# Batch 0 of a fused attention and feed-forward kernel: strided reads for strided writes, fewer constant rows, spare TensorE products, and a new order of steps

## The chip, the cores and the metric

The kernel runs on one core of a Trainium2 chip. Its time is the device time of one execution in microseconds (us); the median of three runs is 301.95 us (301.75 to 302.35). The engines are TensorE (PE in the profile; its weight loads PEld), VectorE (DVE), ScalarE (ACT), GpSimd (POOL) and SyncE (SP, which only issues DMAs here).

## The reference

Four batches of eight heads, 768 positions and 64 features go through block-sparse attention, and its result through a feed-forward layer with softplus. Keys are taken in chunks of 32 (24 chunks). For each query an upper bound on its product with any key of a chunk is worked out from the chunk's smallest and largest key values; the six chunks with the largest bounds, among those not in the future, are kept, and ordinary causal softmax attention runs over them.

```python
k_min, k_max = min, max of k over each chunk of 32
ub = sum_d maximum(q * k_min, q * k_max)          # one bound per query and chunk
ub = where(causal, ub, -1e9); top = 6 largest
scores = where(in a top chunk and causal, scale * q @ k.T, -1e9)
attn = softmax(scores) @ v
x = attn as (3072 tokens, 512)
out = softplus(x @ w_in) @ w_out                  # 512 -> 2048 -> 512
```

The sum of maxima is the same as max(q, 0) times k_max plus min(q, 0) times k_min, and also as max(q, 0) times k_max plus max(-q, 0) times (-k_min).

## The kernel before, in words

The work is cut into units. A unit is a pair of heads of one batch. In batch 0 each pair is halved along the queries, so that the first results come sooner: units 0 to 3 are the first 384 queries of the four pairs, units 4 to 7 the second 384. Units 8 to 19 are whole pairs of batches 1 to 3.

A unit goes through these steps, and each step has a short name that the order of work uses:

- `L` loads q, k or v (SP's queue). `ck`, `cq`, `cv` cast them to bf16.
- `kt` and `qt` transpose k and q on TensorE into PSUM (batch 0 only; later batches use DMA transposes, `fk` and `fq`). For batch 0's k the positions arrive interleaved by four, and the transposed tile holds them as (t, s), where position is 4 s + t.
- `rg` reduces the transposed k to chunk maxima (`.0`) and minima (`.1`), L234; `pk` packs them for TensorE, L240. `qp` and `qn` make max(q, 0) and min(q, 0), L262.
- `kr` copies the transposed k of one head into the score operand `Kaug` (L248). In batch 0 this copy puts the positions back in order: it reads PSUM in one run and writes every fourth element of SBUF.
- `U` is TensorE's bound product (L278, L279) with the causal mask added (L281), `M` takes the eight largest per row (MAX8, L291), `T` writes the selection beside q (L299, L300).
- `a` (batch 0) transposes q together with its selection and copies both to the score operand `Qaug` (L312, L313), reading PSUM in one run and writing every third element. Later batches use `qr` and `s` (L267, L324).
- `S` is a group of score products (L362) with exp on ACT (L366) and a causal cut of the diagonal blocks on POOL (L369). A score operand has 128 rows: 64 of the data and 64 in which the selection meets constant rows in `Kaug`, which drive unselected chunks to a huge negative score.
- `V` multiplies with v (L383, PSUM tile `o_ps`), `n` divides by the row sum (reciprocal L394, product L395), `X` and `x` transpose and copy the result (L402, L410).
- `I` is one step of the first feed-forward product with softplus (tile `hp`, L421; tile `gT`, L429), `F` a quarter of the second (tile `op`, L437), `ob` its copy and store (L442, L444). `I0.0.3` is step 3 of the first half of batch 0; `w` loads the weights on POOL's DMA queue. `tE` and `tP` load the ACT table of exp or of softplus ahead of its use (L122); where the table does not fit the next function, a load is put in.

The letters V, A and G behind a step name the engine (DVE, ACT, POOL). The whole order is written out by hand as text: `ORDER["start"]` for batch 0 and the beginning of batch 1, and `ORDER["cycle"]`, which is run twice. Every engine and every DMA queue takes its instructions strictly in this order. PSUM has three kinds of buffers of two each: `ps_big` (scores and `hp`), `ps_sm` and `ps_w`.

Before the first step a block builds the constants: `aug` (64 rows that hold the chunk pattern, rows 25 to 63 zero) on DVE and POOL, the identity for transposes on POOL, the causal masks, and zeros and ones in several tiles on DVE. `aug_rows(i)` copies all 64 rows of `aug` by DMA, issued by ACT, into the constant half of the two `Kaug` tiles of pair i.

Of the kernel before, what the change touches and what calls it, by code (L numbers as in the profile page):

```python
# [21 lines left out]
L3.k L1.q L1.k L3.q ck1.G L0.k L0.q ck0.V cq1.V kt1.b cq0.V L2.v L3.v kt0 rg1.0 qt0 rg0.1 kr1.1.A qt1.b rg0.0 pk0  # L22
kr0.1.A qp0 rg1.1 L1.v qn0 pk1 qn1 L2.q U0 kr1.0.A kr0.0.A M0 L2.k T0 qp1 a0.1.V a0.0.A ck2.V L0.v U1 cq2.V ar1 cv0.G
M1 S0.0.0 S0.1.0 T1 kt2 cv1 rg2.1 ck3.V rg2.0 a1.0.V a1.1.A V0.0 qt2 V0.1 kr2.0.A cq3.A pk2 S1.0.0 n0.0 qp2 kr2.1.A
qn2 ar2 kt3 rg3.1 w0 L4.q U2 M2 n0.1 S1.1.0 V1.0 qt3 T2 ar3 kr3.0.A n1.0 rg3.0 a2.0.A a2.1.A qp3 cv2.A X0 w1 pk3 V1.1
x0 n1.1 kr3.1.A qn3 cv3 S2.0.0 S2.1.0 U3 M3 X1 L5.q T3 a3.0.A L6.q w2 L5.k x1.A ck5.V V2.0 n2.0 L4.k cq4.A V2.1 a3.1.V
n2.1 S3.0.0 qt4 ck4.V S3.1.0 V3.0 X2 n3.0 L6.k V3.1 x2.V tP n3.1 kt4 L4.v X3 x3.V I0.0.0 kr4.0.V L5.v I0.0.1 rg4.1
rg4.0 L7.q cq5.G w3 qn4 qp4 I0.0.2 pk4 ck6.G U4 L7.v kt5 rg5.1 I0.0.3 M4 kr4.1.V w4 T4 rg5.0 I0.0.4 cv4.V a4.0.V w5 tE
L8.k kr5.1.A kr5.0.A S4.0.0 qt5 kt6 pk5 L6.v qn5 qp5 cv5.V L7.k U5 M5 rg6.1 S4.0.1 a4.1.V I0.0.5 ck7 T5 cq6.G a5.1.V
z1 qt6 I0.0.6 kr6.1.V a5.0.A qp6 I0.0.7 rg6.0 pk6 qn6 L9.v z0 kr6.0.V U6 cq7.G S4.1.0 M6 T6 S4.1.1 V4.0 cv6.G L8.v  # L30
a6.1.V n4.0 L9.k S5.0.0 a6.0.V V4.1 n4.1 S5.0.1 kt7 qt7 cv8.G S5.1.0 rg7.0 L8.q rg7.1 X4 L9.q qn7 cv7.G V5.0 S5.1.1
kr7.0.A pk7 kr7.1.A qp7 n5.0 x4.A cq8.V S6.0.0 ck8.A L10.q U7 S6.0.1 M7 F0.0.0 T7 a7.0.V V5.1 S6.1.0 n5.1 a7.1.V
F0.0.1 S6.1.1 ck9.A F0.0.2 V6.0 S7.0.0 fk8 S7.0.1 cq9.A n6.0 V6.1 cv9.G rg8.0 X5 x5.A n6.1 L10.v L10.k tP F0.0.3 ob0.0
S7.1.0 fk9 V7.0 F0.1.0 n7.0 fq9 F0.1.1 X6 F0.1.2 S7.1.1 F0.2.0 rg9.1 F0.1.3 V7.1 fq8 x6.V ck10.G n7.1 L11.q X7 x7.A
F0.2.1 rg8.1 F0.2.2 qn8 qr9.1.V F0.2.3 I0.1.0 kr8.0.V qr8.0.G ob0.1.V fk10 L11.k qp8 pk8 L11.v U8 ob0.2.V kr8.1.A M8
cq10.V qr8.1.G cv10.V I0.1.1 qp9 kr9.1.G fq10 T8 I0.1.2 I0.1.3 cq11.G I0.1.4 qn9 L12.q cv11.V L12.k s8 I0.1.5 I0.1.6
I0.1.7 rg9.0 L12.v pk9 S8.0.0 qr9.0.V fq11 rg10.0 U9 ck11 tE S8.0.1 L13.k M9 T9 fk11 S8.0.2 rg10.1 L13.v ck12 s9 L13.q
kr10.0.A L14.q S8.1.0 kr9.0.A qp10 qn10 pk10 V8.0 F0.3.0 S8.1.1 U10 kr11.0.G M10 T10 n8.0 qr10.0.G S8.1.2 F0.3.1
S9.0.0 S9.0.1 V8.1 n8.1 cq12.A qr10.1 F0.3.2 cv12.G kr10.1.G rg11.0 S9.0.2 S9.1.0 s10 qr11.0.V rg11.1 X8 F0.4.0 L14.v
qn11 x8.A V9.0 kr11.1.A qp11 fk12 ck13 pk11 qr11.1.G S9.1.1 S9.1.2 n9.0 F0.3.3 fq12 U11 fk13 ob0.3.A M11 T11 L15.v  # L40
S10.0.0 V9.1 S10.1.0 n9.1 S10.0.1 s11 X9 cv13.V kr12.0.G qr12.0 qp12 rg12.0 rg12.1 L14.k S10.0.2 S10.1.1 qr12.1 pk12
V10.0 cq13.V S10.1.2 kr12.1.G L15.k S11.0.0 L15.q F0.4.1 S11.0.1 qn12 x9.V F0.4.2 fq13 S11.0.2 n10.0 U12 S11.1.0 V11.0
M12 S11.1.1 n11.0 V10.1 T12 F0.4.3 ck14.V S11.1.2 cq14.G n10.1 F0.5.0 s12 V11.1 F0.5.1 cv14.G tP n11.1 F0.5.2 X11 X10
F0.5.3 x11.V cv15.A ob0.4.A fk14 L16.q x10.V I1.-.0 I1.-.1 I1.-.2 qn13 rg13.0 I1.-.3 kr14.1.V fq14 L16.k L16.v I1.-.4
qp14 I1.-.5 rg14.1 qn14 qp13 ob0.5.A rg14.0 I1.-.6 I1.-.7 rg13.1 pk14 I1.-.8 kr13.0.V I1.-.9 cq15.A ck15.G qr14.1.V
# [12 lines left out]
M17 I2.-.10 I2.-.11 qn18 T17 I2.-.12 U18 kr18.0 I2.-.13 fq19 cv19.A I2.-.14 I2.-.15 L21.q M18 kr18.1.V tE T18 L21.k
s18 qr18.0.G L21.v s17
# [11 lines left out]
def kernel(  # L71
# [35 lines left out]
    aug = singles.tile([D, S], BF16, name="aug")  # L107
# [39 lines left out]

    def aug_rows(i):
        for e in range(2):
            nc.scalar.dma_start(out=Kaugs[2 * i + e][D * e:D * (e + 1), :], in_=aug)  # L150
# [66 lines left out]

    def k_turn(u, at=(ps_w, "w")):
        p, t0, t1 = units[u]
        st = state[u]  # L220
        st["kT"] = at[0].tile([128, (t1 - t0) * 128], BF16, name="kT", tag=at[1])
        r = (t1 - t0) * 32
        for t in range(4):
            nc.tensor.transpose(st["kT"][:, t * r:(t + 1) * r],
                                st["kb"][:, t].rearrange("p e d -> p (e d)"), ident[0:r, 0:r])

    def k_range(u, which):
# [6 lines left out]
        nc.vector.tensor_reduce(st["km2"][:, which, :], kT, axis=AX.XY, op=(ALU.max, ALU.min)[which])  # L234
# [7 lines left out]
    def k_rows(u, e, copy=nc.vector.tensor_copy):  # L242
# [3 lines left out]
        if t1 - t0 < NT:  # L246
            o, kT = o.rearrange("p (s t) -> p t s", t=4), kT.rearrange("p (t s) -> p t s", t=4)
        copy(o, kT)  # L248

    def q_turn(u, at=(ps_w, "w")):  # L250
        p, t0, t1 = units[u]
        st = state[u]
        st["qT"] = at[0].tile([128, (t1 - t0) * 128], BF16, name="qT", tag=at[1])
        for t in range(t1 - t0):
            nc.tensor.transpose(st["qT"][:, t * 128:(t + 1) * 128],
                                st["row"][:, t, 1:3, :].rearrange("p c d -> p (c d)"), ident)

    def q_sign(u, name):
# [3 lines left out]
        (nc.vector.tensor_scalar_max if name == "qpos" else nc.vector.tensor_scalar_min)(st[name], st["qT"], 0.0)  # L262
# [6 lines left out]
    def bounds(u):  # L269
# [4 lines left out]
        ub = ps_sm.tile([128, n, cs, 2], F32, name="ub", tag="sm")  # L274
# [218 lines left out]
    with tc.manual_schedule():  # L493
# [5 lines left out]
        for m in kmms:  # L499
            nc.vector.memset(m, 0.0)  # L500
# [52 lines left out]
```

## Time and profile before

| what | value |
|---|---|
| median of three runs | 301.95 us |
| the profiled execution: time, span | 301.01 us, 299.2 us |
| busy: PE, DVE, ACT, POOL | 260.1, 171.4, 197.9, 74.4 us |
| mean granted TensorE clock | 0.97 |
| chain that ended last: PE, DVE, ACT, DMA, issue | 62%, 17%, 10%, 5%, 3% of the span |
| first TensorE instruction | 6.92 us |
| first feed-forward product (`hp`) | 36.8 us |
| moved by DMA in the first 60 us | 12.30 MB, 205 GB/s |

How to read it: the page cuts the span into 40 slices of 7.5 us and gives each engine's busy share in tenths. The chain of work that ended last is followed back from the last instruction, at each step to what released it; a row of it in order of time is start, duration, and what ran. In a group by line, `out<-in`, partitions x elements and type are followed by the count, the busy time in us and the mean of one in ns, then the idle time before them and what ended it. A row of stretches is from:to, length, then busy time and count of PE, PEld, DVE, ACT and POOL, the granted TensorE clock (1 is full speed), the DMA share and GB/s.

### The profile page before, as it was taken

The page shows a single profiled execution, that of the slowest core. Times are in us where ns is not written, and L with a number is a line of the kernel's source. Part 1 is how long each engine was busy: PE and PEld are TensorE (multiplying, and loading weights), DVE is VectorE, ACT ScalarE, POOL GpSimd, SP SyncE. Part 2 cuts the span into 40 slices and gives each one's busy share as a digit, 9 for nine tenths or more (in the row PEclk, how much of TensorE's full clock was granted, in tenths as well). Part 3 has the DMA queues.
Part 4 walks back from the last instruction along what each step waited for, and adds up shares of the span by engine and source line. Part 5 has one row for each costly group of instructions (what it writes and reads, how often), then busy time and mean ns, then how long its engine had stood idle before and what let it go on. Part 6 is the DMA issues. An engine that isn't in the chain of part 4 may idle for free.

```text
span 299.2 us, 6118 instructions
## 1 busy us (share of the span) xinstructions
PE 260.1 (87%) x2407; PEld 162.0 (54%) x2432; DVE 171.4 (57%) x572; ACT 197.9 (66%) x244; POOL 74.4 (25%) x104
## 2 busy tenths in 40 slices
PE   0385795789898797799999999999999999999994
PEld 0263553456455464556666666556666655665441
DVE  4986477985485799985459684646494313000000
ACT  1588549899756797655768788765786774567100
POOL 5035412433410665171013324112032120000000
PEclk9996599999999799999999999999999999999999
DMA  7989999916769998519395731932000101000111
GB/s 187 208 202 190 240 201 197 214 37 132 169 103 243 208 199 187 123 53 192 90 182 84 176 101 24 187 101 51 2 3 35 72 2 70 35 2 0 70 72 70
DMA packets 93628, 35.26 MB, mean 118 GB/s; under 512 B 82336, under 2 KB 90528, under 8 KB 93600
## 3 DMA queue, kind: packets, MB, share of 16 engines
q1 hardware_dynamic: 88768, 29.89, 47.9%
q0 software_dynamic: 4192, 4.19, 8.7%
q10 hardware_dynamic: 640, 0.79, 1.1%
q8 instruction: 19, 0.31, 0.5%
q14 instruction: 9, 0.07, 0.1%
HBM read 27.26 MB, written 6.29 MB: 112 GB/s over the span
## 4 chain that ended last, share of the span: by engine, by line
PE 62%; DVE 17%; ACT 10%; DMA 5%; issue 3%; SPq 1%; POOL 0%; ACTq 0%; DVEq 0%
PE hp L421 23%; PE op L437 21%; PE sc L362 8%; PE o_ps L383 6%; ACT attnT L366 4%; DVE km L234 3%; DMA vf<-in_v_dram 3%; ACT Kaug L248 2%; DMA kf<-in_k_dram 2%; DVE m L291 2%; PE x_ps L402 1%; DVE on L395 1%; DVE Kaug L248 1%; DVE kmm L240 1%; DVE Qaug L313 1%
## 5 line engine op out<-in xcount | busy, mean ns | idle before, releaser
L366 ACT ACTIVATE attnT<-sc 128x1024 bf16<-128x1024 f32 (+2 forms) x96 | 84.6, 917 | 23.0 <-PE sc L362 21.9
L437 PE MATMUL op<-w_out_sb,gT 128*128 128x512 bf16 x360 | 88.6, 381 | 1.4 <-issue 0.2
L421 PE MATMUL hp<-xT,w_in_sb 128*128 128x384 bf16 x512 | 87.0, 328 | 1.3 <-ACT attnT L366 1.3
L429 ACT ACTIVATE gT<-hp 128x768 bf16<-128x768 f32 x64 | 51.9, 810 | 38.6 <-PE hp L421 38.5
L421 PEld LDWEIGHTS <-w_in_sb 128*128 128x128 bf16 x512 | 49.9, 99 | 34.2 <-issue 2.7
L369 POOL TENSOR_SCALAR_AFFINE_SELECT attnT<-attnT 128x768 bf16<-128x768 bf16 (+1 forms) x40 | 29.4, 737 | 121.2 <-ACT attnT L366 121.1
L362 PE MATMUL sc<-Qaug,Kaug 128*128 128x128 bf16 (+3 forms) x399 | 53.1, 266 | 3.6 <-ACT attnT L366 2.1
L437 PEld LDWEIGHTS <-gT 128*128 128x128 bf16 x384 | 36.0, 98 | 35.0 <-issue 0.6
L362 PEld LDWEIGHTS <-Kaug 128*128 128x128 bf16 x400 | 30.3, 102 | 17.5 <-issue 4.0
L383 PE MATMUL o_ps<-vaug,attnT 128*128 128x65 bf16 x672 | 28.9, 198 | 4.5 <-ACT Qaug L313 2.0
L442 DVE COPY ob<-op 128x512 f32<-128x512 f32 x14 | 9.6, 686 | 40.0 <-PE op L437 39.8
L383 PEld LDWEIGHTS <-attnT 128*128 128x128 bf16 x672 | 26.7, 100 | 10.6 <-issue 3.1
L234 DVE TENSOR_REDUCE km<-kT_sb 128x24 bf16<-128x768 bf16 x24 | 22.2, 946 | 3.4 <-DMA kT_sb<-kb 3.2
L324 DVE COPY Qaug<-sT 64x768 bf16<-64x768 bf16 x24 | 13.3, 553 | 13.6 <-PE sT L321 13.4
L395 DVE TENSOR_TENSOR on<-o_ps,rr 128x384 bf16<-128x384 f32 (+1 forms) x40 | 19.1, 478 | 1.4
L394 DVE RECIPROCAL rr<-o_ps 128x6 f32<-128x6 f32 (+1 forms) x40 | 7.4, 184 | 20.5 <-PE o_ps L383 20.3
L281 DVE TENSOR_TENSOR ubm<-ub,causal 128x288 f32<-128x288 f32 (+2 forms) x20 | 7.5, 380 | 18.5 <-PE ub L279 18.2
L442 ACT COPY ob<-op 128x512 f32<-128x512 f32 x10 | 5.9, 585 | 17.2 <-PE op L437 17.2
L248 ACT COPY Kaug<-kT 64x384 bf16<-64x384 bf16 x12 | 11.8, 1024 | 7.5 <-DVE km L234 7.3
L291 DVE MAX8 m<-ubm 128x8 f32<-128x12 f32 (+3 forms) x192 | 16.4, 160 | 0.5
L278 PE MATMUL ub<-kmm,qpos 128*128 128x48 bf16 (+1 forms) x96 | 7.8, 184 | 6.2 <-DVE kmm L240 2.2
L410 ACT COPY xT<-x_ps 128x768 bf16<-128x768 bf16 (+1 forms) x11 | 7.6, 689 | 7.5 <-PE x_ps L402 7.4
(69 smaller groups left out, 243.5 us busy)
## 6 DMA issues: line engine op xcount, KB each, us to landing
out_dram<-ob SPq DMA_DIRECT2D x24, 256.0 KB, 2.1
kf<-in_k_dram SPq DMA_DIRECT2D x12, 384.0 KB, 6.1
vf<-in_v_dram SPq DMA_DIRECT2D x12, 384.0 KB, 5.4
qf<-in_q_dram SPq DMA_DIRECT2D x12, 384.0 KB, 5.4
w_in_sb<-in_moe_w_in_dram POOLq DMA_DIRECT2D x4, 512.0 KB, 8.0
w_out_sb<-in_moe_w_out_dram POOLq DMA_DIRECT2D x2, 1024.0 KB, 16.5
kf<-in_k_dram SPq DMA_DIRECT2D x8, 192.0 KB, 4.2
qf<-in_q_dram SPq DMA_DIRECT2D x8, 192.0 KB, 4.2
```

The lines of the kernel that those rows point to most:

```text
L234: nc.vector.tensor_reduce(st["km2"][:, which, :], kT, axis=AX.XY, op=(ALU.max, ALU.min)[which])
L248: copy(o, kT)
L291: nc.vector.max(out=m8[:, t, e, :], in_=ubm[:, t, 0:max(8, 4 * (t + 1)) if n == NT else cs, e])
L362: nc.tensor.matmul(sc[:, o:o + (z - a) * 128], pair[p]["Ka"][e][:, tj * 128:(tj + 1) * 128], pair[p]["Qa"][e][:, a * 128:z * 128], start=T ...
L366: nc.scalar.activation(at[:, g * 1024:g * 1024 + n], sc[:, 0:n], ACT.Exp, scale=scale)
L369: nc.gpsimd.affine_select(out=diag, in_=diag, compare_op=ALU.is_ge, fill=0.0, base=0, channel_multiplier=-1, pattern=[[0, t1 - t0], [1, 128]])
L383: nc.tensor.matmul(o_ps[:, t, :], at[:, o:o + 128], pair[p]["va"][:, tj, e, :], start=(tj == 0), stop=(tj == t0 + t))
L395: nc.vector.tensor_tensor(st["on"][:, :, e, :], o_ps[:, :, 0:D], rr.to_broadcast([128, n, D]), op=ALU.mult)
L421: nc.tensor.matmul(hp[:, n, 0:HALF], w_in_sb[:, dt, ft * 128:(ft + 1) * 128], xT[b][:, dt, half * HALF:(half + 1) * HALF], start=(dt == 0) ...
L429: nc.scalar.activation(o, hp[:, :, 0:HALF], ACT.Softplus)
L437: nc.tensor.matmul(held[b, stt], gT[b][:, ft, stt * 128:(stt + 1) * 128], w_out_sb[:, ft, :], start=(ft == 0), stop=(ft == KFF - 1))
L442: copy(ob, held.pop((b, stt)))
```

## The change

- The two strided copies of batch 0 are turned round: they write SBUF in one run and read PSUM with jumps (`kr`: 96 elements between neighbours; `a`: 128 elements).
- `aug` has 32 rows, of which 25 go to `Kaug` by DMA; the rest of the constant half is zeroed by a POOL memset before each DMA.
- Minima are negated in the reduce, and `qn` makes max(-q, 0), so that both signs can also run on ACT as a Relu (`qp7.A`, `qn11.A` and others).
- `D n.m` adds n to a counter, and the next PSUM tile that TensorE starts (`kT`, `qT`, `ub`, `qa_ps`, `sc`, `o_ps`, `x_ps`) is first written by that many products of the identity with itself, transposes where the tile is bf16. There are 140 of them: 49 ahead of the first transpose of k, none in `ORDER["cycle"]`.
- Several steps name the PSUM buffer that they use (`.s`, `.w`, `.b`).
- The constants become steps (`C`), and the whole order of steps is written anew, loads included (`L1.q L1.k L0.k` first, where it was `L3.k L1.q L1.k`).

```diff
-L3.k L1.q L1.k L3.q ck1.G L0.k L0.q ck0.V cq1.V kt1.b cq0.V L2.v L3.v kt0 rg1.0 qt0 rg0.1 kr1.1.A qt1.b rg0.0 pk0
...
+L1.q L1.k L0.k Ci Ca Cr1.V cq1.V ar0 Cc Cr0.V L0.q L1.v Cv.V ck1.G D48.2 cq0.V D1.16 ck0.V L3.q kt1.b L3.k kt0 L2.v
...
+cv2.G pk3 a2.0.A.s D1.19 X0 x0.A V1.1.s qp3.V n1.1 w1 D1.22 qn3 L6.q kr3.1.A D1.31 S2.0.0 S2.1.0 D1.28 D6.40 U3.s M3
+D1.27 X1.b x1.A L5.q w2 D9.26 T3 D13.21 D1.30 cv3 L5.k D1.29 a3.0.A L4.k S3.0.0 L6.k ck5.V V2.0 V2.1 a3.1.V.w n2.0
...
+kr4.0.V I0.0.1 L5.v L7.q rg4.1 cq5.G I0.0.2 ck6.V qp4 L8.k w3 qn4 L6.v pk4 U4.s kt5 cv4.V D1.39 kr5.1.A I0.0.3 kr4.1.V
+L7.v rg5.1 tE M4 I0.0.4 w5 T4 D1.48 qt5 rg5.0 L7.k a4.0.V.s S4.0.0 qn5.V kr5.0.A S4.0.1 w4 cv5.V D1.41 kt6 qp5.V pk5
...
-    aug = singles.tile([D, S], BF16, name="aug")
+    aug = singles.tile([32, S], BF16, name="aug")
...
     def aug_rows(i):
         for e in range(2):
-            nc.scalar.dma_start(out=Kaugs[2 * i + e][D * e:D * (e + 1), :], in_=aug)
+            nc.gpsimd.memset(Kaugs[2 * i + e][D * e:D * (e + 1), :].bitcast(F32), 0.0)
+        for e in range(2):
+            nc.scalar.dma_start(out=Kaugs[2 * i + e][D * e:D * e + NCH + 1, :], in_=aug[0:NCH + 1, :])
...
+    def keep_busy(ps):
+        n = min(128, ps.shape[1])
+        for _ in range(spare[0]):
+            if ps.dtype == BF16:
+                nc.tensor.transpose(ps[:, 0:128], ident, ident)
+            else:
+                nc.tensor.matmul(ps[:, 0:n], ident, ident[:, 0:n], start=True, stop=True)
+        spare[0] = 0
...
-        nc.vector.tensor_reduce(st["km2"][:, which, :], kT, axis=AX.XY, op=(ALU.max, ALU.min)[which])
+        nc.vector.tensor_reduce(st["km2"][:, which, :], kT, axis=AX.XY, op=(ALU.max, ALU.min)[which],
+                                negate=which == 1)
...
-            o, kT = o.rearrange("p (s t) -> p t s", t=4), kT.rearrange("p (t s) -> p t s", t=4)
+            o, kT = o.rearrange("p (s t) -> p s t", t=4), kT.rearrange("p (t s) -> p s t", t=4)
...
+        sign = 1.0 if name == "qpos" else -1.0
+        if on == "A":
+            nc.scalar.activation(st[name], st["qT"], ACT.Relu, scale=sign)
+        elif sign > 0:
+            nc.vector.tensor_scalar_max(st[name], st["qT"], 0.0)
+        else:
+            nc.vector.tensor_scalar(st[name], st["qT"], -1.0, 0.0, ALU.mult, ALU.max)
...
-        copy(Qa[e][:, t0 * 128:t1 * 128].rearrange("p (s t) -> p t s", t=t1 - t0),
-             qa_ps.rearrange("p (t s) -> p t s", t=t1 - t0))
+        copy(Qa[e][:, t0 * 128:t1 * 128].rearrange("p (s t) -> p s t", t=t1 - t0),
+             qa_ps.rearrange("p (t s) -> p s t", t=t1 - t0))
```

## The prediction, made before the changed kernel ran

> **What bounds the kernel now.** I read the page's slices first, then stretches of the span, then the chain of work that ended last, then the groups by line with the shapes kept apart. On the page:
>
> ```profile
> span 299.2 us, 6118 instructions
> PE 260.1 (87%) x2407; PEld 162.0 (54%) x2432; DVE 171.4 (57%) x572; ACT 197.9 (66%) x244; POOL 74.4 (25%) x104
> ...
> PE   0385795789898797799999999999999999999994
> ...
> PEclk9996599999999799999999999999999999999999
> DMA  7989999916769998519395731932000101000111
> ```
>
> From slice 17 (126 us) TensorE is full. I cut the stretches where the granted clock changes:
>
> ```profile
> 0.00:14.94 14.94, 3.16 (x26) 2.12 (x27) 9.81 (x40) 5.70 (x7) 4.55 (x12) 1.00 0.88 197
> ...
> 25.18:38.83 13.65, 9.96 (x88) 7.10 (x87) 8.13 (x29) 7.91 (x12) 6.30 (x10) 0.50 1.23 221
> 38.83:100.28 61.45, 50.44 (x496) 31.49 (x498) 44.87 (x146) 49.03 (x58) 17.40 (x27) 1.00 0.90 164
> 100.28:103.69 3.41, 3.19 (x30) 1.98 (x27) 2.68 (x7) 2.32 (x3) 1.90 (x3) 0.50 0.97 163
> ...
> 126.00:299.20 173.20, 167.93 (x1462) 101.50 (x1476) 76.79 (x253) 106.89 (x134) 28.81 (x33) 1.00 0.32 73
> ```
>
> The first number after the length is TensorE's busy time. Behind 126 us it leaves 5.3 us of 173 free, so a gain must come from the 126 us before, where 33.8 us are idle and some work runs at clock 0.50. No engine is full there (the second stretch of 61 us: PE 82%, VectorE 73%, ScalarE 80%): the chain hops from engine to engine. The chain in order of time shows the copies that the change touches:
>
> ```profile
> 14.12 0.81 DVE Qaug L313
> ...
> 23.16 1.00 ACT Kaug L248
> 24.18 1.44 ACT Qaug L313 x2
> ...
> 47.16 1.01 ACT Kaug L248
> 48.18 1.01 ACT Kaug L248
> ```
>
> Besides these it holds L313 at 17.73, 29.37, 45.60, 51.95 and 58.77, and L248 at 52.77, 55.91, 64.01 and 65.03: 8 copies of L313 (4 on DVE, 4 on ACT) and 7 of L248 (5 ACT, 2 DVE).
>
> **Copies with the stride on the read (new L286, L361).** Their rows, beside contiguous ones of 384 elements:
>
> ```profile
> L248 ACT COPY Kaug<-kT 64x384 bf16<-64x384 bf16 x12 | 11.8, 1024 | 7.5 <-DVE km L234 7.3
> L313 DVE COPY Qaug<-qa_ps 128x384 bf16<-128x384 bf16 x10 | 8.0, 801 | 3.3 <-PE qa_ps L312 3.3
> L313 ACT COPY Qaug<-qa_ps 128x384 bf16<-128x384 bf16 x6 | 4.6, 804 | 2.1 <-PE qa_ps L312 2.0
> L248 DVE COPY Kaug<-kT 64x384 bf16<-64x384 bf16 x4 | 4.1, 1014 | 0.1
> L394 DVE RECIPROCAL rr<-o_ps 128x3 f32<-128x3 f32 x16 | 2.8, 174 | 6.2 <-PE o_ps L383 6.2
> L410 ACT COPY xT<-x_ps 128x384 bf16<-128x384 bf16 x4 | 2.0, 490 | 1.7 <-PE x_ps L402 1.7
> L410 DVE COPY xT<-x_ps 128x384 bf16<-128x384 bf16 x4 | 1.4, 353 | 0.7 <-PE x_ps L402 0.7
> ```
>
> ACT and DVE pay the same for the same stride (1.02 and 1.01; 0.80 and 0.80) although they differ without one (0.49 and 0.35): what costs is the strided write, not the engine. No row reads PSUM two bytes at a time with a jump each time, so I bound it. Lower end: the contiguous 0.49 and 0.35. Upper end: L394 reads one element in 65 and takes 174 ns for 3, 191 for 6: 5.7 ns per element, 384 x 5.7 + 0.15 = 2.3 us, arithmetic of the reciprocal included. Nearest are L234, which jumps after every 8 elements, and the MAX8 of L291, which reads every second one (158 ns for 12, 171 for 24), both at about 1 ns per element. I take one element at a time: 0.49 on ACT; on DVE 0.55, from 686 ns for 512 f32 (L442) and 357 for 192 (L395), 1.03 ns per element. On the chain: 4 x 0.26 + 4 x 0.31 + 5 x 0.53 + 2 x 0.47 = 5.9 us. Two thirds pass through, as DVE, ACT and PE are busy 72, 66 and 60% of the first 60 us and another path is soon late: **-3.9**.
>
> The Trainium skill, "Advanced Engine Details and Errata", PSUM Cachelines, speaks against this step: PSUM lines hold 8 bytes, and two consecutive elements should be contiguous for the best rate. No row here reads so; by that rule these copies would be the rival at half rate below.
>
> **Spare products and the clock.** The clock changes at 25.18, 38.83, 100.28 and 103.69 us: gaps of 4, 22 and 1 times 3.41. On this grid lies 21.77 too, where three transposes (L255) fall from 0.51 to 0.33 us; so before it TensorE ran slow as well, though the record says 1.00. The stretch 18.35 to 21.76 held some 3,150 columns, which a slow array (1,536 columns of sc in 1.28 us: 1.2 per ns) takes 2.6 us for, 77% of it, and the clock rose; 14.94 to 18.35 held 69% and it did not; 21.76 to 25.18 held 25% of a fast one's and it fell. PE pieces of the chain while slow: 3.1 us (14.94 to 21.76), 7.3 (25.18 to 38.83), 2.9 (100.28 to 103.69), 13.3 in all; the same groups take about two thirds when fast (0.50 to 0.33; o_ps x6 0.49 to 0.34), so 4.4 us are to be had at most and 0 at least. 49 of the 140 spares stand before the first transpose, 28 round the selection of unit 3, 22 near the end of batch 0; most others singly, 0.05 to 0.1 us in a step of 3.41. I take half: **-2.2**.
>
> The price: the first 49 x 0.107 = 5.2 us start when the identity is ready, about 1.4 us now that it is POOL's first constant, and end at 6.7; the first transpose began at 6.92, and its key cast still stands behind POOL's constants (rows add up to 6.6). Uncovered, they would cost 5.2. The other 91 take 4.9 us fast, 9.7 slow, mostly ahead of a product that waits for DVE or ACT (18.4 us of PE idle before 40 us hide them): 0 to 9.7, taken at **+0.7**.
>
> The Trainium skill, "TensorE: Matmul & The Clock Gate", Part 4, says that transposes do not count as TensorE-busy in the same way. Nearly all spares are transposes, so by it only the rival on the clock is left. The trace leaves it open: without transposes the steps above held 58% (rose) and 41% (did not).
>
> **Constant rows.** 8 DMAs of 25 rows in place of 64 move 0.48 MB less, 2.3 us at 205 GB/s; but 0.00 to 14.94 is bounded by latency: with the new load order I walk the DVE queue to the first selected row at 13.5 us, as now (13.52). Taken at 0 (at best -1). The memsets, 8 x 0.44 (L135: 330 ns for 288 elements) on POOL, lie in its idle time; uncovered they cost up to 3.5. But a wait is added: the third and fourth pair of ACT's DMA issues wait for memsets that stand behind POOL's diagonal masks. The fourth comes one copy (0.49) after an exp whose mask (0.52) and memsets (0.88) are still to do; queued behind it are the two query copies of unit 2. **+0.3** (0 to 0.9).
>
> **Table loads.** The built program has 17 ACT_TABLE_LOADs for 15, 1283 ns each. The warm-up tE now stands between I0.0.3 and I0.0.4, so the fifth softplus loads its table again and the scores of unit 4 load exp again: 2.6 us on ACT around 40 us, less the 0.5 to 0.8 that ACT idles before each gT there. hp and sc share two PSUM buffers, so TensorE is next late. **+1.5** (0 to 2.6).
>
> **Signs.** Negation inside the reduce and the two-step qneg keep their row (0.35 us). Seven sign ops go to ACT, all after 60 us: DVE gains some 2.9 us, ACT pays 5.5 (0.83 for 768 elements), mostly beside a full TensorE: 0, from -1 to +2.
>
> **Order.** Behind unit 0, DVE's new list from unit 1's bounds (14.4 us) to unit 3's selected rows, with no wait in it, is 2.2 us to unit 1's rows, 5.9 to unit 2's (reduces 3 x 0.55, copy 0.55, cast 0.42, signs and pack 1.07, norms 2 x 0.53, bounds, MAX8s and select 1.18) and 3.9 to unit 3's: 26.4 for 28.8 now, at best. That includes copies and clock, which give 1.5 to 2 by then; what it has beyond them, through to the first hp, I take at **-1.0** (-3 to +3). SP's queue takes L1.q first and batch 1's loads in a new order behind freed buffers. DMA is nearly full to 56 us, so being more than the 2.3 us saved ahead there can turn into waiting for loads; that is why I add no more.
>
> Sum: -3.9 - 2.2 + 0.7 + 0.3 + 1.5 - 1.0 = -4.6. The profiled execution took 301.01 us (1.8 outside the span); this makes 296.4, and with the 0.94 by which the median stands above it, **297.3 us**.
>
> **Rivals.**
> - Strided PSUM reads at half rate: 0.81 on ACT, 0.95 on DVE. The copies term shrinks to 4 x 0.14 - 5 x 0.21 - 2 x 0.07 = -0.6, of which -0.4; all -1.1: 300.9. For it: no row. Against: L291's stride costs nothing. 13%.
> - Slower: the read jump costs more than the write stride did. Without copies the terms leave -0.7, so it decides once the 15 copies grow by 0.07 us each. At 1.4 us, midway between 0.55 and 2.3: 8 x 0.6 + 7 x 0.38 = 7.5, of which 5.0: 306.2; at 2.3 us, 315. For it: L394. 15%.
> - The spares do not hold the clock, so the change doesn't do what it says: -2.2 is lost: 299.5. For it: steps of 25% are far from 77%. 15%.
> - All passes through: copies -5.9, clock -4.4, order -3, loads and spares +1: 289.7. For it: 33.8 us of idle time. 17%.
> - The forecast: 40%.
>
> 80% range: 289.5 to 304.0, which takes in the half-rate reads and table loads fully on the path, and cuts the far end of the slow case. Under 0.2% (0.6 us) no measurement here can tell a change: faster 0.77, same 0.06, slower 0.17.
>
> **What would show it.** Copies: L286 and L361 at 0.49 to 0.55; near 0.97 their gain is gone. Clock: granted 1.00, and three transposes at 0.33, between 25 and 39 us. Table loads: three of them around a single softplus near 40 us. The first hp before 34 us, unit 3's mask before 31. TensorE's busy time behind batch 0 unchanged. A wait of several us for a load between 40 and 60 us would break the forecast, as would copies over 1 us.

## The result, and the profile after

The changed kernel takes 303.49 us (median of 13 runs, 303.09 to 304.92); the kernel before took 302.37 beside it. Ratio **1.0045**, interval 1.0024 to 1.0066: a little slower, where the forecast was 297.3. The profiled execution took 303.38 us with a span of 301.7, so 2.4 us more than that of before. The times and ratios below are of runs in the chip's usual state; two of e15's twelve, at 307.2 and 307.3 us, were slower and are left out.

The page of the changed kernel, the same lines that were shown of before:

```profile
span 301.7 us, 6417 instructions
PE 267.4 (89%) x2547; PEld 171.4 (57%) x2572; DVE 165.5 (55%) x563; ACT 200.6 (66%) x260; POOL 73.9 (24%) x107
...
PE   7376595969989796899999999999999999999994
...
PEclk9675988799999999999999999999999999999999
DMA  7969999935699994995664562631201110100111
```

DVE is busy 5.9 us less (5.0 of it the copies), TensorE 7.3 us more (the 140 spares among it). From 126 us on TensorE leaves 5.6 us of 175.7 free, as before:

```profile
126.00:301.70 175.70, 170.11 (x1488) 102.84 (x1504) 76.60 (x254) 111.70 (x142) 29.07 (x34) 1.00 0.33 76
```

So the difference was made earlier. The groups by line, shapes kept apart, to 110 us show the copies:

```profile
L286 ACT COPY Kaug<-kT 64x384 bf16<-64x384 bf16 x12 | 5.6, 474 | 7.9 <-DVE kmm L278 7.7
...
L361 DVE COPY Qaug<-qa_ps 128x384 bf16<-128x384 bf16 x9 | 4.9, 554 | 5.8 <-PE qa_ps L360 5.8
...
L169 POOL MEMSET Kaug<- 64x384 f32 x8 | 3.4, 419 | 0.2
L361 ACT COPY Qaug<-qa_ps 128x384 bf16<-128x384 bf16 x7 | 3.2, 477 | 5.8 <-PE qa_ps L360 5.8
...
L286 DVE COPY Kaug<-kT 64x384 bf16<-64x384 bf16 x4 | 2.2, 555 | 0.1
```

They are what was taken, 0.47 on ACT and 0.55 on DVE, beside 1.02 and 0.80 before. And yet the first feed-forward product starts at 38.76 us (before: 36.78), and the step I0.0.5 at 51.95 (50.28). Between these the stretches show something new. The granted clock changes here at 9.21, 19.45, 22.87, 29.69, 36.52, 39.93, 50.17 and 57.00 us, all whole steps of 3.41 us apart; the grid starts at another time in every execution. Cut on it, TensorE is busy only 1.33 us from 46.76 to 50.17, and then runs two steps at clock 0.50.

```profile
46.76:50.17 3.41, 1.33 (x16) 0.85 (x14) 2.01 (x7) 3.35 (x5) 0.00 (x0) 1.00 1.20 195
50.17:53.59 3.42, 2.17 (x17) 1.21 (x15) 1.89 (x10) 3.36 (x5) 1.37 (x2) 0.50 1.11 235
53.59:57.00 3.41, 3.41 (x17) 1.99 (x16) 1.58 (x3) 2.35 (x3) 0.50 (x1) 0.50 0.97 161
```

The eight `hp` products that start at 51.95 take 2.72 us there; before, at full clock, the same eight took 1.46.

ScalarE's instructions in order of time say what TensorE waited for (start, duration, what ran):

```profile
45.94 1.28 ACT L125 ACT_TABLE_LOAD   x1
47.24 0.21 ACT L125 ACTIVATE dummy<-dummy 1x8 f32<-1x8 f32 x1
47.46 1.28 ACT L480 ACT_TABLE_LOAD   x1
48.76 0.81 ACT L480 ACTIVATE gT<-hp 128x768 bf16<-128x768 f32 x1
49.59 1.28 ACT L415 ACT_TABLE_LOAD   x1
```

Three table loads stand around one softplus: 3.84 us of loads for 0.81 of work.

### The profile page after: what moved, and what is told of

The parts are those of the page before. It is cut to its first block, busy times and chain, and to the rows that moved or that the text cites. A ratio compares the mean times of both kernels' runs of the same rounds, so it can differ in the third digit from the quotient of the medians.

```text
span 301.7 us, 6417 instructions
## 1 busy us (share of the span) xinstructions
PE 267.4 (89%) x2547; PEld 171.4 (57%) x2572; DVE 165.5 (55%) x563; ACT 200.6 (66%) x260; POOL 73.9 (24%) x107
## 4 chain that ended last, share of the span: by engine, by line
PE 71%; DVE 10%; ACT 10%; issue 3%; DMA 2%; POOL 1%; SPq 1%; ACTq 0%; DVEq 0%
PE hp L472 27%; PE op L488 23%; PE sc L411 9%; PE o_ps L433 6%; ACT attnT L415 4%; DMA kf<-in_k_dram 2%; PE x_ps L453 2%; DVE kmm L278 1%; ACT L415 1%; PE sT L369 1%; DVE qpos L306 1%; PE qa_ps L360 1%; DVE km L271 1%; ACT gT L480 1%; ACT L125 1%
## 5 line engine op out<-in xcount | busy, mean ns | idle before, releaser
L415 ACT ACTIVATE attnT<-sc 128x1024 bf16<-128x1024 f32 (+3 forms) x96 | 83.8, 913 | 17.4 <-PE sc L411 16.7
L472 PE MATMUL hp<-xT,w_in_sb 128*128 128x384 bf16 x512 | 89.1, 332 | 1.3 <-ACT attnT L415 1.3
L411 PE MATMUL sc<-Qaug,Kaug 128*128 128x128 bf16 (+3 forms) x396 | 50.5, 259 | 5.7 <-ACT attnT L415 2.3
L411 PEld LDWEIGHTS <-Kaug 128*128 128x128 bf16 x400 | 29.4, 100 | 18.1 <-issue 5.8
L433 PE MATMUL o_ps<-vaug,attnT 128*128 128x65 bf16 x672 | 28.0, 195 | 7.3 <-POOL attnT L418 4.7
L433 PEld LDWEIGHTS <-attnT 128*128 128x128 bf16 x672 | 25.3, 99 | 12.2 <-POOL attnT L418 7.3
L493 DVE COPY ob<-op 128x512 f32<-128x512 f32 x12 | 8.1, 685 | 39.4 <-issue 23.0
L493 ACT COPY ob<-op 128x512 f32<-128x512 f32 x12 | 7.1, 589 | 18.9 <-PE op L488 18.9
L461 ACT COPY xT<-x_ps 128x768 bf16<-128x768 bf16 (+1 forms) x9 | 5.9, 658 | 8.8 <-PE x_ps L453 8.7
L278 DVE COPY kmm<-km 64x48 bf16<-64x48 bf16 (+1 forms) x40 | 11.1, 277 | 0.6
```

The lines of the kernel that those rows point to most:

```text
L278: copy(km[e * D:(e + 1) * D, :, 4 * t0:4 * t1, e], state[u]["km2"][e * D:(e + 1) * D])
L411: nc.tensor.matmul(sc[:, o:o + (z - a) * 128], pair[p]["Ka"][e][:, tj * 128:(tj + 1) * 128], pair[p]["Qa"][e][:, a * 128:z * 128], start=T ...
L415: nc.scalar.activation(at[:, g * 1024:g * 1024 + n], sc[:, 0:n], ACT.Exp, scale=scale)
L433: nc.tensor.matmul(o_ps[:, t, :], at[:, o:o + 128], pair[p]["va"][:, tj, e, :], start=(tj == 0), stop=(tj == t0 + t))
L472: nc.tensor.matmul(hp[:, n, 0:HALF], w_in_sb[:, dt, ft * 128:(ft + 1) * 128], xT[b][:, dt, half * HALF:(half + 1) * HALF], start=(dt == 0) ...
L493: copy(ob, held.pop((b, stt)))
```

## The experiments

Two theories stood at first. **Order**: the turned copies gain what was forecast, and the new order of steps loses more. **Copies**: they gain little, because another path is late at once. Times are medians, ratios are to the kernel before on the same chip, over five rounds; they need not be the quotients of the medians (e9 and e10 have the same time and 1.0030 and 1.0007). First hp is the start of the first feed-forward product in the profile. e1 to e4, e5 to e8, e9 to e12, e13 to e16 and e17 with e18 were taken together; between such sets, which ran on different chips or at another time, the ratio compares better than the time. Where two intervals overlap, the difference is not settled.

| run | what it is | us | ratio (interval) | first hp, us |
|---|---|---|---|---|
| e1 | before + turned copies | 297.84 | 0.9867 (0.982 to 0.991) | 35.14 |
| e2 | changed, old copies | 310.41 | 1.0281 (1.023 to 1.033) | 42.29 |
| e3 | changed, no spares | 305.09 | 1.0107 (1.006 to 1.016) | 39.13 |
| e4 | changed, tE later | 300.47 | 0.9942 (0.991 to 0.998) | 39.13 |
| e5 | changed code, old order | 301.98 | 1.0029 (1.000 to 1.006) | 39.40 |
| e6 | e5 + spares | 301.43 | 1.0012 (0.998 to 1.004) | 40.53 |
| e7 | changed, scores up | 305.64 | 1.0152 (1.011 to 1.019) | 39.63 |
| e8 | e1, scores down | 300.77 | 0.9985 (0.996 to 1.001) | 36.40 |
| e9 | changed, 64 rows by DMA | 303.08 | 1.0030 (1.000 to 1.006) | 38.50 |
| e10 | changed, memsets early | 303.08 | 1.0007 (0.998 to 1.004) | 37.21 |
| e11 | e9 + tE later | 299.59 | 0.9891 (0.984 to 0.994) | 36.80 |
| e12 | e11 + scores up | 298.85 | 0.9875 (0.984 to 0.992) | 37.29 |
| e13 | e5, 64 rows by DMA | 298.59 | 0.9894 (0.986 to 0.993) | 35.84 |
| e14 | e5, memsets early | 299.79 | 0.9928 (0.990 to 0.996) | 36.92 |
| e15 | changed, spares at the loads | 302.44 | 1.0014 (0.998 to 1.005) | 38.69 |
| e16 | e13 + spares | 297.73 | 0.9873 (0.984 to 0.990) | 36.11 |
| e17 | e14, 32 rows by DMA | 298.83 | 0.9914 (0.988 to 0.995) | 34.96 |
| e18 | changed, all finds, 32 rows | 297.78 | 0.9871 (0.983 to 0.991) | 36.45 |

### e1 and e2: the copies alone, and all but the copies

e1 changes two lines of before (e2 turns the same two back in the changed kernel):

```diff
-            o, kT = o.rearrange("p (s t) -> p t s", t=4), kT.rearrange("p (t s) -> p t s", t=4)
+            o, kT = o.rearrange("p (s t) -> p s t", t=4), kT.rearrange("p (t s) -> p s t", t=4)
...
-        copy(Qa[e][:, t0 * 128:t1 * 128].rearrange("p (s t) -> p t s", t=t1 - t0),
-             qa_ps.rearrange("p (t s) -> p t s", t=t1 - t0))
+        copy(Qa[e][:, t0 * 128:t1 * 128].rearrange("p (s t) -> p s t", t=t1 - t0),
+             qa_ps.rearrange("p (t s) -> p s t", t=t1 - t0))
```

> The kernel before with one edit: the copies into Kaug and Qaug of batch 0 (L248, L313) read with the stride. In the profile of the changed kernel they took 0.47 on ACT and 0.55 on DVE. Theory 1 (the copies are worth what the chain said, and something else in the change, its order of steps first, gives it back): 2 to 4 us faster than before. Theory 2 (the copies were not what set the end, because another engine's work was as late): within 0.6 us of before.

> The changed kernel with only the copies turned back (stride on the write). Theory 1: 2 to 4 us slower than the changed kernel, so 3 to 5 us slower than before. Theory 2: as the changed kernel, some 1 us slower than before.

The copies gain 4.3 us by themselves (297.84 beside 302.15) and 6.9 in the new order (310.41 to 303.49), both more than the 2 to 4 us expected. Why they are worth more in the new order was not tried; e2's trace has 34 us at clock 0.50 before 126 us, the changed kernel's 27. The theory "copies" falls. Everything else together loses some 5.7 us in the presence of the copies.

### e3: no spares

Every `D` is taken out of the order.

> The changed kernel without the 140 spare TensorE products. Theory 1 (the order is at fault): within 0.6 us of the changed kernel, the spares win at the clock about what they cost. Theory 3 (the spares stand in the path of real products): 1 to 2 us faster than the changed kernel. If the spares do what they are for, 1 to 3 us slower than it, with the clock at 0.50 between 29 and 36 us where the changed kernel shows 1.00.

The spares gain 1.6 us (the intervals of the two ratios, up to 1.0066 and from 1.0058, just overlap). Whether they warm the array, which means that it runs at its fast clock, can be read from the transposes, TensorE in order of time. In the changed kernel:

```profile
1.43 4.97 PE L245 MATMUL kT<-ident 128*128 128x128 bf16 x49 [1.43 <-POOL ident masks.py:199]
6.83 0.34 PE L261 MATMUL kT<-ident,kb 96*128 96x96 bf16 x4 [0.43 <-POOL kb L212]
...
7.62 0.50 PE L294 MATMUL qT<-ident,row 128*128 128x128 bf16 x6
...
29.95 0.33 PE L453 MATMUL x_ps<-ident,on 128*128 128x128 bf16 x3
...
31.45 0.33 PE L360 MATMUL qa_ps<-ident,row 128*128 128x128 bf16 x3
```

In e3, the same view:

```profile
6.86 0.82 PE L261 MATMUL kT<-ident,kb 96*128 96x96 bf16 x8 [6.86 <-POOL kb L212]
7.48 0.84 PE L294 MATMUL qT<-ident,row 128*128 128x128 bf16 x6
...
29.56 0.48 PE L453 MATMUL x_ps<-ident,on 128*128 128x128 bf16 x3 [0.16 <-ACT attnT L415]
...
30.94 0.50 PE L360 MATMUL qa_ps<-ident,row 128*128 128x128 bf16 x3 [0.91 <-DVE row L347]
```

Six transposes take 0.50 us behind the 49 spares and 0.84 without: the array is fast then, though both records say 1.00 there. At 9.21 us it falls again. Between 29.69 and 36.52 us it is fast once more: three transposes take 0.33 us, where e3's take 0.48 to 0.51. The Trainium skill, "TensorE: Matmul & The Clock Gate", Part 4, says that transposes do not count as TensorE-busy in the same way; this trace disagrees, for nothing but transposes had run before those six.

### e4 and e15: the table loads

```diff
-L7.v rg5.1 tE M4 I0.0.4 w5 T4 D1.48 qt5 rg5.0 L7.k a4.0.V.s S4.0.0 qn5.V kr5.0.A S4.0.1 w4 cv5.V D1.41 kt6
+L7.v rg5.1 M4 I0.0.4 tE w5 T4 D1.48 qt5 rg5.0 L7.k a4.0.V.s S4.0.0 qn5.V kr5.0.A S4.0.1 w4 cv5.V D1.41 kt6
```

> The changed kernel with the warm-up tE moved one softplus later, behind step I0.0.4, as before: 15 table loads in place of 17. Theory 1: 2 to 4 us faster than the changed kernel (2.6 us of loads, and the slow clock from 50.6 to 57 us that follows TensorE's wait for them), so 1 to 3 us faster than before. If ACT has room there: within 0.6 us of the changed kernel.

One word moved by two places: 3.0 us. The stretches of e4, cut on its own grid, show why it is more than the 2.6 us of loads: TensorE stays busy and the clock up.

```profile
45.74:49.15 3.41, 2.76 (x25) 1.73 (x23) 3.31 (x15) 2.53 (x4) 0.00 (x0) 1.00 1.21 195
49.15:52.56 3.41, 2.85 (x32) 1.85 (x30) 2.65 (x14) 3.35 (x6) 1.36 (x2) 1.00 1.20 233
```

e15 leaves the loads and fills the hole: `D12.0` ahead of `S4.0.0`, `D20.41` for `D1.41` ahead of `kt6`.

> The changed kernel with its three table loads and with 31 more spare products: 12 ahead of unit 4's first scores, 20 (for 1) ahead of unit 6's key transposes, where TensorE waits for ACT. TensorE was busy 1.58 of the 3.41 us from 47.18 to 50.59, and the clock fell at 50.59 for two steps. If a good part of the cost of the loads is that fall: granted clock 1.00 from 50 to 58 us, and 301.3 to 302.3 us beside 303.5. If it is ACT's 2.6 us alone: the clock holds or not, the time stays within 0.7 us of 303.5.

The 1.58 us and the fall at 50.59 in this text come from stretches cut 0.42 us beside the changed kernel's grid; on it they are 1.33 us and 50.17. The stretches of e15, on its own grid:

```profile
47.36:50.77 3.41, 1.97 (x28) 1.55 (x26) 1.67 (x6) 3.35 (x5) 0.00 (x0) 1.00 1.22 219
50.77:54.19 3.42, 3.06 (x41) 2.37 (x39) 1.97 (x11) 3.34 (x6) 1.64 (x3) 1.00 1.21 226
```

With 1.97 us in place of 1.33 the clock held, and the hp run that stood at 87.05 us stands at 84.84: the fall costs 2.2 us there. In e4 it stands at 83.70, so the loads themselves cost another 1.1. At the end 0.7 is left of it, because this run, unlike the changed kernel's, has a slow stretch at 102 to 105 us. The times (ratio 1.0014 beside 1.0045) overlap in their intervals: the mechanism is shown by the trace, its worth in the end is not settled.

### e5, e6, e13, e14, e17: the constant rows in the old order

e5 puts the order of before into the changed code; ahead of it stand the constants:

```diff
+Ca Ci Cc Cm.V Cr0.V Cr1.V Cv.V ar0
```

> The changed kernel's code (turned copies, 25 constant rows with POOL memsets, negated minima, PSUM homes) with the order of steps of the kernel before, its constants built first in the old sequence, no spares and no step moved to another engine. Beside the turned copies alone (297.84 us, 15 ACT_TABLE_LOADs) only the rows and the negations are new. Theory A (the loss lies in the order of steps, most of it before the first feed-forward product): within 1 us of 297.84. Theory B (the constant rows cost: POOL's memsets and the waits of ACT's DMA issues for them delay the key copies): 299.5 us or more, first hp later than 36 us.

The loss is there without the new order: 4.1 us more than e1. ScalarE and POOL in e5, in order of time, in the stretch of units 1 and 2, and the DVE instruction that waits for them:

```profile
23.48 0.81 ACT L413 ACTIVATE attnT<-sc 128x768 bf16<-128x768 f32 x1 [2.09 <-PE qa_ps L358]
...
24.43 0.51 POOL L416 TENSOR_SCALAR_AFFINE_SELECT attnT<-attnT 128x384 bf16<-128x384 bf16 x1 [1.25 <-ACT attnT L413]
24.90 0.88 POOL L167 MEMSET Kaug<- 64x384 f32 x2
25.34 1.50 ACTq L169 DMA_DIRECT2D Kaug<-aug  x2
...
26.89 0.47 ACT L284 COPY Kaug<-kT 64x384 bf16<-64x384 bf16 x1 [2.60 <-DMA Kaug<-aug]
...
27.39 0.56 DVE L269 TENSOR_REDUCE km<-kT 128x12 bf16<-128x384 bf16 x1 [4.08 <-ACT Kaug L284]
```

This is a chain that leaves ACT and comes back to it: the exp (ACT) frees POOL's mask, the mask the memset behind it, the first memset the DMA issue on ACT's queue, and behind the issue stands ACT's key copy, for which DVE waits 4.08 us. e13 takes the memsets away and brings 64 rows again:

```diff
         for e in range(2):
-            nc.gpsimd.memset(Kaugs[2 * i + e][D * e:D * (e + 1), :].bitcast(F32), 0.0)
-        for e in range(2):
-            nc.scalar.dma_start(out=Kaugs[2 * i + e][D * e:D * e + NCH + 1, :], in_=aug[0:NCH + 1, :])
+            nc.scalar.dma_start(out=Kaugs[2 * i + e][D * e:D * (e + 1), :], in_=aug)
```

> The old order in the new code (301.98 us) with one part undone: 64 constant rows by DMA, no memsets. If the rows made its loss (ACT's issues for pairs 2 and 3 wait for memsets behind POOL's masks): within 1 us of the turned copies alone, ratio to before 0.985 to 0.990, first hp from 39.4 back to 35 to 36 us. If the negations or the sequence of the constants did: ratio stays over 0.996.

The same place in e13, ScalarE in order of time, has the issue beside the exp:

```profile
21.62 0.81 ACT L411 ACTIVATE attnT<-sc 128x768 bf16<-128x768 f32 x1 [0.34 <-PE sc L407]
22.18 1.12 ACTq L167 DMA_DIRECT2D Kaug<-aug  x2
...
23.34 0.47 ACT L282 COPY Kaug<-kT 64x384 bf16<-64x384 bf16 x1 [0.91 <-DVE on L441]
```

That is 3.4 us of time (301.98 to 298.59) and 3.6 us of first hp: the rows made e5's loss. By the ratios it is 1.35%, 4.1 us. What is left to e1, 0.27% with overlapping intervals, falls to the negations and the sequence of constants together.

e14 keeps 25 rows and only moves the memsets of pairs 1 to 3 ahead of `M0`; e17 does that with 32 rows (the last seven are zero):

> The old order in the new code with 25 rows by DMA, the memsets of pairs 1 to 3 moved ahead of unit 0's selection. If the wait for POOL made the loss: the issues of pairs 2 and 3 start at 19.5 to 22 us again, first hp 35 to 37 us, ratio 0.985 to 0.992. If the longer issue (0.75 for 0.56 us each) did: ratio over 0.994.

> The old order with early memsets (e14, ratio 0.9928) and 32 constant rows in place of 25 in each DMA. If 25 rows are an awkward number for the issue, one issue falls from 0.70 to about 0.49 us, as with 64 rows, and the ratio to 0.987 to 0.991 (64 rows without memsets: 0.9894). If the issue is longer because ACT's queue handles the memset's semaphore at each, it stays 0.70 and the ratio at 0.993. The Trainium skill, DMA: Bandwidth & Descriptors, Why a DMA increments its semaphore by 16 and not by 1, says that such a DMA is spread over the largest number of engines up to 16 that divides its rows, 5 for 25 and 16 for 32 or 64; by it the first case holds.

e14 wins back 2.2 us, so most of it was the wait for POOL. The issues of 25 rows still take 0.70 us each (median of 8), those of 64 rows 0.49, those of 32 rows 0.53 (e17). So it is the number 25 and not the memset that makes the issue longer. The Trainium skill, "DMA: Bandwidth & Descriptors", Why a DMA increments its semaphore by 16 and not by 1, has the rule: 25 rows are spread over 5 engines, 32 and 64 over 16, and what is missing to 16 the issuing sequencer counts itself. The section gives no price for that; the durations fit it. The gain in time (1.0 us, intervals overlap) is not settled.

e6 and e16 add 80 spares to e5 and to e13 (`Ci` first, `D49.0` ahead of `kt1`, `D7.0` ahead of `U3`, `D24.0` ahead of `a3.0`):

> The same with spares in the old order: identity built first, 49 transposes ahead of the first transpose of k, 7 products ahead of unit 3's bounds and 24 ahead of its first query transpose. The changed kernel without its spares took 1.6 us more than with them, so theory C (spares are worth as much in any order) says 1 to 2 us below the run without them. Rival D (the spares only fill a hole that the new order makes): the first 49 make the first transposes fast and the clock falls again at the next step, as in the changed kernel, the other 31 are too few, and the time is within 0.7 us of the run without spares or above it.

> The version that the runs point to: old order, turned copies, 64 rows by DMA, 49 + 7 + 24 spares. In the old order spares gained 0.5 us (301.43 beside 301.98), so 297 to 298 us, ratio 0.982 to 0.988. If it is over 0.992, the spares cost there: 49 transposes delay the first transpose of k.

0.5 and 0.9 us, both inside the intervals: in the old order the spares bring little or nothing.

### e7 and e8: the scores moved up and down

e7 moves three steps of the changed kernel up; e8 moves the first two down in e1:

```diff
-M1 S0.0.0 T1 kt2 D1.13 D1.14 D1.10 rg2.1 rg2.0 a1.0.V D1.11 S0.1.0 a1.1.A V0.0
+M1 S0.0.0 S0.1.0 T1 kt2 D1.13 D1.14 D1.10 rg2.1 rg2.0 a1.0.V D1.11 a1.1.A V0.0
...
-pk2 qn2 kr2.0.A D1.15 kt3 n0.0 ar2 L4.q D1.17 rg3.1 U2 w0 M2 cq3.A S1.1.0 S1.0.0
+pk2 S1.0.0 qn2 kr2.0.A D1.15 kt3 n0.0 ar2 L4.q D1.17 rg3.1 U2 w0 M2 cq3.A S1.1.0
...
-ck5.V V2.0 V2.1 a3.1.V.w n2.0
+ck5.V a3.1.V.w V2.0 V2.1 n2.0
```

> The changed kernel with three steps moved in the text and nothing else: unit 0's second score group directly behind its first (it stood behind unit 1's selection and query transposes), unit 1's first score group ahead of unit 2's bounds (it stood behind them), unit 3's second query transpose ahead of unit 2's products with v. Theory A1 (TensorE is served strictly in the order of the text, so scores that are ready wait behind a product that waits for DVE): unit 0's second exp moves from 18.7 to about 17.8 us, unit 1's first exp from 22.6 to about 20, first hp from 38.8 to 36 to 37.5 us, time 301.0 to 302.5 beside 303.5. Theory B (the start costs, not the scores): first hp stays within 0.5 us of 38.8 and the time within 0.7 us of 303.5.

> The counter-test: the kernel before with the turned copies (297.84 us) and two score groups moved down to where the new order has them: unit 0's second behind unit 1's selection and first query transpose, unit 1's first behind unit 2's bounds. Theory A1: first hp from 35.1 to 36.5 to 38 us, time 299 to 301. Theory B: no change beyond 0.7 us.

e8 loses 2.9 us, as expected. **e7 was a miss**: 2.2 us slower, not 1 to 2.5 faster. Its unit 0 exps do come at 16.65 us (the second was at 18.68), but unit 1's first exp at 20.20 now puts its mask (21.08) ahead of pair 2's memset (21.55), and the issue moves from 20.47 to 21.99. The theory that the order alone loses fell with this run; the chain over POOL, found in e5, took its place.

### e9 to e12 and e18: the finds in the new order

e9 has e13's edit in the changed kernel, e10 has e14's. e11 is e9 with e4's edit, e12 adds e7's. e18 has 32 rows, early memsets, and the edits of e4 and e7.

> The changed kernel with one part undone: all 64 constant rows come by DMA again, without POOL's memsets. Theory B2 (ACT's DMA issues for pairs 2 and 3 wait for memsets that POOL can start only behind the mask of the exp before, and hold ACT 0.75 us each where 64 rows took 0.56): the issues leave 20.5 and 25.1 us, the exps of units 1 and 2 move up by 1 to 2 us, first hp from 38.8 to 36.5 to 37.8, time 300 to 302 beside 303.5. Rival A (the order of scores and selections alone): first hp within 0.5 us of 38.8, time 303 to 304.

> The changed kernel with the memsets of pairs 1 to 3 issued together on POOL before unit 0's selection (POOL idle from 9 to 17 us), 25 rows by DMA as before. If the loss of the rows is the wait for POOL: as good as the run with 64 rows by DMA (300 to 302), or better by the bytes saved. If it is the longer issue (4 pairs, 0.4 us each): the issues of pairs 2 and 3 still take 1.50 us, and the time stays 0.5 to 1.5 us above that run.

> Both finds undone in the changed kernel: 64 rows by DMA, and the exp warm-up behind I0.0.4 (15 table loads). If the two losses add: 303.5 - 3 - (the gain of 64 rows alone, 1.5 to 3.5) = 297 to 299, as the turned copies in the old order (297.84). If the new order loses by itself, it stays above 299.5.

> The same with the scores and unit 3's query transpose moved up. With the memsets this move cost 2 us, because unit 1's exp and its mask came ahead of pair 2's memset, and ACT's DMA issue waited 1.5 us longer for it. Without memsets that coupling is gone: theory A1 expects 1 to 2 us less than the run without the move (295.5 to 298); if the move still costs, the loss was not this coupling.

> The changed kernel with all finds: 32 rows by DMA with early memsets, the exp warm-up behind I0.0.4, the scores and unit 3's query transpose moved up. With 64 rows by DMA this order gave 0.9875 of before. If the bytes saved count for anything, 0.983 to 0.986; if the early DMA traffic is not what bounds, 0.986 to 0.989, equal to the old order with the turned copies (0.9867).

By themselves the rows win 0.4 us (e9), inside the intervals and a miss; e10, 303.08 too, missed its 300 to 302. e10 shows where a gain can go: its first hp is 1.55 us earlier than the changed kernel's, and at 61 us it still leads by 1.2. Then, in the stretches of e10 on its grid:

```profile
58.29:61.70 3.41, 1.56 (x35) 1.35 (x36) 2.88 (x11) 3.09 (x4) 2.94 (x5) 1.00 1.21 194
61.70:65.12 3.42, 3.42 (x37) 2.74 (x34) 2.54 (x8) 2.07 (x3) 1.51 (x4) 0.50 0.46 88
```

1.56 us busy of 3.41, and again a fall. The score products that start at 62.86 us in the changed kernel start at 61.68 here; those that wait next for an exp start at 66.51 and 66.52: the lead is gone. e9's profile has another reason as well, its fourth pair's two issues held ACT 1.91 us where e11, the same to that point, had 1.08; why is open. With both gone (e11) the kernel is 0.9 us faster than with the loads alone gone (e4, overlapping intervals) and 3.5 faster than with the rows alone gone (e9). e12's move is worth 0.7 (overlapping intervals), where with the memsets it cost 2.2: what e7 ran into was that chain. It missed the 1 to 2 us expected; in the old order the same place of the scores cost 2.9 (e8).

e12 and e18 take 298.85 and 297.78 us. With e1 and e16 they are four versions at ratios 0.9867 to 0.9875, all faster than both kernels and not told apart. e18 came out as expected if the bytes that 32 rows save do not count.

## Why the prediction was wrong, point by point

Two terms of the sum failed, both in what a small step does beyond its own engine: the table loads and the wait for the constant rows. The other terms came out right in size or cannot be told from right.

- **Copies, -3.9: right.** -4.3 alone, -6.9 in the new order. That two thirds of the 5.9 us on the chain pass through was a guess, and that it fitted the old order so well is partly luck: in the new order more than all of it came. The reads cost some 1.2 ns per element on ACT and 1.4 on DVE with all fixed time in it; the upper bound from the reciprocal was far off. The Trainium skill, "Advanced Engine Details and Errata", PSUM Cachelines, asks for two neighbours to be contiguous for the best rate: on ACT this trace does not show it (0.47 us with jumps, 0.49 without), on DVE it does in part (0.55 beside 0.35). The rivals of half rate and of a dear read are out, and with them the mechanism of the slower side.
- **Clock and spares, -2.2 + 0.7: right in sum.** -1.6 (e3); in the old order only 0.5 and 0.9 (e6, e16). The clock was up for half of the stretch named: slow from 22.87 to 29.69 us, fast to 36.52, slow to 39.93. Some of the working was off: from 38.83 to 100.28 us it is 18 steps, not 22; the slow PE pieces before 21.76 add up to 4.0 us, not 3.1; and of the 140 spares 95 are transposes, not nearly all. The working also missed how little idle time brings a fall. It counted the step ahead of the fall at 25.18 as 25% of a fast array's columns; by busy time that step is at 47% (1.60 of 3.42 us). The 20 profiles, each cut on its own grid from the step ahead of its first recorded fall to 126 us, show this: all 47 steps at full clock that were busy 45% or less were followed by a fall, none of the 382 above 58% was, and of the 38 between 14 were. In the changed kernel 58% was followed by a fall and 47% was not:

```profile
19.45:22.87 3.42, 1.97 (x31) 1.30 (x29) 3.08 (x13) 2.16 (x6) 2.16 (x4) 1.00 1.04 240
60.41:63.83 3.42, 1.61 (x30) 1.44 (x31) 2.92 (x12) 2.56 (x3) 2.96 (x6) 1.00 0.69 113
```

What decides in between is open. Of the slow steps, none of the 44 busy under 82% was followed by a rise, and 61 of the 63 above were.
- **Constant rows, 0, and the wait that they add, +0.3 (0 to 0.9): the wait was found and mis-sized, the first step that failed.** I priced the fourth pair alone, by what ACT idles, and took issues at the old length. In the old order rows and wait cost 3.4 us (e5 to e13; 4.1 by the ratios), most of it the wait (e14), because ACT's key copy stands behind the issue and DVE waits for it. In the new order they cost 0.4 to 0.9 (e9, e4 to e11), inside the intervals.
- **Table loads, +1.5 (0 to 2.6): the second step that failed.** 3.0 (e4) to 3.5 us (e9 to e11), past the upper end. I counted ACT's time and put TensorE next late; that TensorE's idle time drops the clock for the two 3.41 us steps behind it was not in the sum, though the price of a slow clock was worked out further up. e15, where the loads stay and the clock holds, puts that at 2.2 us by 85 us; how much of it lasts to the end is open.
- **Order, -1.0 (-3 to +3): the times were wrong, the term is not refuted.** I walked DVE's list "with no wait in it" and had unit 3's selected rows at 26.4 us; they come at 31.0. DVE's waits of the changed kernel to 60 us (waiter, released by, us, times, longest):

```profile
DVE ubm L328 <- PE ub L326: 5.7, 4, 2.0
...
DVE Qaug L361 <- PE qa_ps L360: 4.8, 3, 2.4
...
DVE rr L444 <- PE o_ps L433: 4.1, 3, 1.8
...
DVE km L271 <- ACT Kaug L286: 1.7, 1, 1.7
```

So other engines make the list's time. What the order is worth depends on what it meets. e12 beside e16 has the two orders with copies and rows alike, loads at 15 and scores up (140 spares and 80): 0.9875 and 0.9873, so about 0, and the intervals leave room for -1.0. e4 beside e6 has them with the rows and memsets of the change and loads at 15: 0.9942 and 1.0012, so the new order is 0.70%, 2.1 us, better, and the intervals do not overlap. It seems to hide part of the rows' wait; no run tests that by itself. It is later in the start (first exp 16.5 us in e12, 15.74 in e16); which step does that was not tried.
- **Signs, 0:** no run contradicts it; with the constants' sequence they are within 0.27% (e13 beside e1), and the intervals leave room for some 0.8%. The sign operations on ACT are part of the new order and were not tried apart.

The ratios make a path from before to the changed kernel: copies -1.33% (e1), negations and constants +0.27 (e13), rows with memsets +1.35 (e5), spares -0.17 (e6), order -0.70 (e4), loads +1.03 (the changed kernel). On another path, over e13, e16, e12, e11 and e4, the rows cost 0.51 and the order with the scores' place 0.18. Each of these parts is uncertain by some 0.5. One percent is 3.0 us, so rows and loads together cost 4.6 to 7.2 us where the sum had +1.8: that turned the gain into a small loss. How the loss is shared between the rows and the order depends on the path.

Undoing the loads, the rows and the scores' place takes the changed kernel from 303.49 to 298.85 us (e12): 4.6 us, about what the forecast had promised from the whole change.

## What to carry to other kernels

A DMA issue, or any instruction that waits on another engine, belongs to the queue that issues it: list what that other engine has ahead of the release, and what stands behind the issue, before calling the new work hidden. An idle stretch of the array has a second price one step later: here every 3.41 us step at full clock that was busy 45% or less, and some up to 58%, was followed by at least one step at clock 0.50, and that can swallow a gain made earlier. The grid has to be found anew in every profile. In a hand-written order with three engines passing one chain, a walk along a single queue gives a lower bound and not a forecast, and what one part costs depends on which of the others are in place.

## What the runs showed of the hardware

- Strided SBUF writes of two-byte elements cost 1.02 us (every fourth) and 0.80 us (every third) per 384 elements on either engine; PSUM reads with jumps cost ACT nothing (0.47 beside 0.49 contiguous) and DVE 0.20 us (0.55 beside 0.35).
- An issue on ACT's DMA queue takes 0.70 us for 25 rows, 0.53 to 0.56 for 32 (e17, e18), 0.49 to 0.52 for 64 (e13, e9; medians of 8).
- The clock's record says 1.00 from the start, while the array is slow until its first rise: six transposes 0.84 us, 0.50 behind 49 spare ones.
- The clock changes on a grid of 3.41 us whose start differs between executions. Full-clock steps busy 45% or less were followed by a fall (47 of 47), those above 58% were not (0 of 382), those between in 14 of 38 cases.
- At clock 0.50 eight `hp` products take 2.72 us in place of 1.46, three transposes 0.50 in place of 0.33.
